# A bucket pass that shares its one-hot matrices between VectorE, TensorE and ScalarE, and a first hop in 128 columns

## Chip, cores and metric

One core of one Trainium2 chip. The metric is the device time of one execution in microseconds (us), the median of several runs. PE is TensorE, DVE is VectorE, ACT is ScalarE, POOL is GpSimd and SP is SyncE, whose queue issues most of the DMAs.

## What is computed

A graph of N = 10000 nodes with E = 160000 random edges and D = 128 features. Seven hops propagate the features over the edges; a small attention block then runs over the eight values of each node.

```python
h = x
toks = [x]
for _ in range(7):
    msg = h[src] * deg_inv_sqrt[src, None] * deg_inv_sqrt[dst, None]
    h = _segment_sum(msg, dst, N)
    toks.append(h)
tok = jnp.stack(toks, axis=1)                      # (N, 8, D)
...                                                # attention over the 8 tokens of a node
return jnp.einsum('nk,nkd->nd', alpha, o)
```

The change touches only how the edges are sorted and how the first hop is summed.

## The kernel before

**Sorting.** Gather and scatter are done as matrix products with one-hot matrices. For this the edges are bucketed twice. The first pass (`pass_a`) sorts them by destination block, 79 blocks of 128 nodes. The second pass sorts each block's edges by source block: 72 cells with 32 slots each, in 18 groups of four cells (NG = 18), and one more group of four cells (NI = 1) for the sources of the last blocks, so NJ = 19 groups of 128 slots. Edges that don't fit go through an overflow list.

**The second pass, in quads.** Four destination blocks make a quad; there are 20. `place` sorts a quad in two pairs of blocks. For each pair DVE makes the one-hot `oh` of the source cells (L417), PE counts with 25 identity matmuls into `ur` (L421), ACT copies the counts as `H` (L422), four triangular matmuls sum them (L427), ACT copies this as `U` (L429), DVE multiplies `ux` (L219), 16 + 1 matmuls add (L223, L224), DVE reduces to the ranks `rk` (L227), makes the one-hot of the rank `rob` and two products `R` with the source and the destination row (L434, L435), and 50 matmuls put both into the table `tb` (L440), which ACT copies to `tbs` (L441). Then the quad's source rows are stored to DRAM (`srow`, L450), PE spreads the destination rows over partitions with small selection matmuls (L454), ACT copies them as `dsl` (L458), DVE takes the indices `oidx` (L459), and the overflow list is made with `po`, `ph`, two one-hots `ohp` (L484) and matmuls (L487), ending in `lo` and `Sov` (L490 to L494).

**`matrices`** makes the matrices of a block in one fp8 tile `w` of 128 x 4736: 18 groups of gather matrices by comparing `rb` with the partition's number (L511; `rb` is the block's `srow` row on all 128 partitions, loaded at L504 into a pool with one buffer), and 19 scatter matrices of 128 x 128 by comparing `dsl` with a running number (L514). `w` is stored to DRAM for the later hops (L516).

**`hop1` and `block`** use `w` at once for the first hop. For each of nine pairs of groups, `gather` issues eight matmuls that write 32 partitions each into a PSUM tile `p` (L580; pool of three banks), and the tile is copied to `eb`, by ACT (L585) except in the last quad, where it is shared with DVE (L587). A table row is 256 columns wide, two f16 halves whose sum is the value. `scat` multiplies the scatter matrices with `eb` into `acc` (L556), 256 columns and one of ones, which counts in-degrees. `fetched` does it for rows that POOL fetched by indirect DMA (L542). `close` adds the two halves with a DVE reduction into `s` (L571), and `fin1` and `token_out` read `s` (L652, L623).

**The order.** The main loop runs `place` of quad q+1, `matrices` of quad q and `hop1` of quad q-1 side by side. A scheduler then orders the instructions of each engine at build time; on the chip each engine takes them strictly in that order. Hops 2 to 7 load `w` from DRAM and run only `block`.

Of the kernel before, what the change touches and what calls it, by code (L numbers as in the profile page):

```python
# [35 lines left out]
KO = 8  # L36
BIG = 32768.0


class Hops:  # L40
    def __init__(self, ctx, dp, missing, tab, tc, x, src, dst, dis):
# [9 lines left out]
        self.srow = dp.tile([NTP, 4 * NG * CAP], F16, name="srow")  # L51

# [51 lines left out]
        self.mx = [cp.tile([128, NT], F32, name=f"mx{i}") for i in range(2)]  # L104
        self.ctok = [cp.tile([128, NT], F32, name=f"ctok{i}") for i in range(2)]
        self.c1 = [cp.tile([128, NT], F32, name=f"c1{i}") for i in range(2)]
# [289 lines left out]
    def pb_open(self, c):  # L396
        tc, V = self.tc, self.nc.vector
        self.bwp = c.enter_context(tc.tile_pool(name="bw", bufs=2))
        self.bw1 = c.enter_context(tc.tile_pool(name="bw1", bufs=1))
        self.pU = c.enter_context(tc.tile_pool(name="pU", bufs=1, space=PSUM))  # L400
        self.psm = c.enter_context(tc.tile_pool(name="psm", bufs=1, space=PSUM))

        cp = self.bp
        es = cp.tile([NS, 4, NJ], I32, name="es")
        self.nc.gpsimd.iota(es, pattern=[[1, 4], [4, NJ]], base=0, channel_multiplier=-1)
        self.esel = cp.tile([NS, 4, NJ], F16, name="esel")
        V.tensor_scalar(self.esel, es, 0.0, None, op0=ALU.is_equal)

    def place(self, ts, got):
# [41 lines left out]
        dsl = wp.tile([128, 4, NJ], F16, name="dsl")  # L451
        for g in range(n):
            for q in range(4):
                T.matmul(msc[32 * q:32 * q + 32, 32 + g * NJ:32 + (g + 1) * NJ], tbs[:, g, CAP:2 * CAP], self.esel[:, q, :],  # L454
                         start=True, stop=True, tile_position=(0, 32 * q))
                T.matmul(msc[32 * q:32 * q + 32, 16 + g * NI:16 + (g + 1) * NI], tbs[:, g, 0:CAP], self.esel[:, q, NG:],
                         start=True, stop=True, tile_position=(0, 32 * q))
        A.copy(dsl[:, :n, :], msc[:, 32:32 + n * NJ].rearrange("p (g j) -> p g j", j=NJ))  # L458
# [38 lines left out]
    def matrices(self, ts, dsl, W):  # L497

        nc, V = self.nc, self.nc.vector

        def row(t):
            rb = self.bw1.tile([128, 4 * NG * CAP], F16, name="rb")
            r1 = self.srow[t:t + 1, :]
            nc.sync.dma_start(rb, bass.AP(tensor=r1.tensor, offset=r1.offset, ap=[[0, 128], [1, 4 * NG * CAP]]))  # L504
            return rb

        rb = row(ts[0])
        yield
        for g, t in enumerate(ts):
            w = self.gsp.tile([128, (NJ + NG) * 128], F8, name="w")  # L510
            V.tensor_scalar(w[:, NJ * 128:], rb, self.pid1, None, op0=ALU.is_equal, saturate=False)  # L511
            if t != ts[-1]:
                rb = row(t + 1)
            V.tensor_tensor(w[:, :NJ * 128].rearrange("p (j d) -> p j d", d=128), dsl[:, g, :, None].to_broadcast([128, NJ, 128]),  # L514
                            self.iof1[:, None, :].to_broadcast([128, NJ, 128]), op=ALU.is_equal, saturate=False)
            nc.sync.dma_start(self.GSd[t], w)  # L516
            W.append(w)
            yield
# [11 lines left out]
    def block(self, t, w, tab, og, pend, lag, runs, first, evac, fin, lead=False, late=False, mid=None, ahead=None,  # L530
# [5 lines left out]
        m = 257 if first else 256  # L536
        acc = []


        def fetched(i, start=False, stop=False):  # L540
            W = w[:, (NG + i) * 128:(NG + i + 1) * 128] if i < NI else self.Sov[:, t, :]
            T.matmul(acc[0][:, :256], W, og[i], start=start, stop=stop)  # L542
            if first:
                T.matmul(acc[0][:, 256:257], W, self.ones16, start=False, stop=False)
# [6 lines left out]
        def scat(e, jj):  # L551
            if not acc:
                acc.append(self.pacc.tile([128, 512], F32, name="acc", tag="acc"))
            for j in range(e.shape[1]):
                J = 2 * jj + j
                T.matmul(acc[0][:, :m], w[:, J * 128:(J + 1) * 128], e[:, j, :m], start=first and J == 0,  # L556
                         stop=J == NG - 1 and not (first or late))
                if first and J == 0 and not lead:
                    for i in range(NI):
                        fetched(i)  # L560

        def close():
            if first:
                if lead:
                    for i in range(NI):
                        fetched(i)
                T.matmul(acc[0][:, 256:257], self.Sov[:, t, :], self.ones16, start=False, stop=False)
            if first or late:
                T.matmul(acc[0][:, :256], self.Sov[:, t, :], og[NI], start=False, stop=True)  # L569
# [59 lines left out]
    def run(self, ctx, att, nhop=K):  # L629
        tc, nc, V, A, T, G = self.tc, self.nc, self.nc.vector, self.nc.scalar, self.nc.tensor, self.nc.gpsimd  # L630
        with ExitStack() as c:
# [16 lines left out]
            def fin1(t, s, acc):  # L648
                V.tensor_copy(self.indeg[:, t:t + 1], acc[:, 256:257])  # L649
# [48 lines left out]
        with ExitStack() as c:  # L698
# [5 lines left out]
            self.sp = c.enter_context(tc.tile_pool(name="sp2", bufs=2))  # L704
            self.more_ebufs(c.enter_context(tc.tile_pool(name="eb2", bufs=1)), 9, False)
# [592 lines left out]
```

## Time and profile before

| | |
|---|---|
| median of 3 runs | 3991.8 us (3988.98 to 3993.97) |
| the profiled execution | 3999.62 us, its span 3997.8 us |
| mean granted TensorE clock | 0.973 |
| busy over the span | PE 94%, DVE 83%, ACT 68%, POOL 44% |
| first pass | about 0 to 370 us |
| second pass with the first hop | about 370 to 1190 us |
| hops 2 to 7 | about 1190 to 3310 us |
| attention | to the end |

A row of a group gives the line, the engine, the operation, the tiles (out<-in), the shapes and the count; behind the first bar the busy time in us and the mean of one in ns; behind the second the idle time of the engine just before these instructions and what ended it. A row of a timeline gives the start in us, the length in us, and in brackets the idle time before it. A row of the waits gives the total in us, how often, and the longest. A row of the windows gives the start and end of a stretch, its length, then busy us and instructions of PE, PEld (weight loads), DVE, ACT and POOL, the granted clock, the DMA share and GB/s.

### The profile page before, as it was taken

The numbers are of one execution on the slowest core, as the hardware profiler recorded it, in microseconds if no ns is written. First come the engines' busy times: TensorE is split into PE (matmuls) and PEld (weight loads), VectorE is DVE, ScalarE is ACT, GpSimd is POOL, SyncE is SP. The second block draws the span as 40 slices with busy tenths as digits, with TensorE's granted clock in tenths as the row PEclk, the third lists the DMA queues.
The fourth block names the chain that finished last, engine by engine and source line by source line (L and its number), as shares of the span: only waits on it lengthen the run. The fifth ranks groups of instructions, "written<-read, shape, count | busy, mean of one in ns | idle before, by whom it ended". The sixth has DMA issues, their size and how long they took to land.

```text
span 3997.8 us, 165094 instructions
## 1 busy us (share of the span) xinstructions
PE 3745.5 (94%) x69690; PEld 3031.4 (76%) x69690; DVE 3322.9 (83%) x6961; ACT 2724.5 (68%) x6830; POOL 1766.6 (44%) x2342
## 2 busy tenths in 40 slices
PE   6886799999989999999999999999999999999997
PEld 4665566666658888888888788878878887788885
DVE  8998999999977777777777777777766666999998
ACT  6884456666666666666666666666665658888884
POOL 0000333333335665666666566656656662222222
PEclk8998899999999999999999999999999999999998
DMA  3100445454556666666666666666656552222220
GB/s 104 32 2 1 134 151 154 149 162 143 156 168 189 201 201 193 202 203 200 193 202 202 185 202 202 202 189 198 202 184 205 186 183 77 74 74 76 78 78 13
DMA packets 321189, 594.93 MB, mean 149 GB/s; under 512 B 56183, under 2 KB 214101, under 8 KB 315189
## 3 DMA queue, kind: packets, MB, share of 16 engines
q1 hardware_dynamic: 282485, 506.62, 40.0%
q0 software_dynamic: 35392, 72.55, 6.3%
q8 instruction: 546, 8.95, 0.9%
q10 hardware_dynamic: 2560, 5.12, 0.4%
q14 instruction: 206, 1.69, 0.1%
HBM read 455.43 MB, written 128.67 MB: 146 GB/s over the span
## 4 chain that ended last, share of the span: by engine, by line
PE 71%; DVE 19%; ACT 4%; issue 2%; DMA 2%; POOL 0%; another core or an unknown queue 0%; SPq 0%; DVEq 0%; ACTq 0%; POOLq 0%
PE p L580 26%; PE acc L556 24%; PE acc L542 4%; DVE w L514 3%; PE pv L972 3%; PE po L983 3%; PE pu L961 3%; DVE ux L219 2%; DVE o L212 2%; ACT rs L340 2%; PE tb L440 2%; PE pt L951 1%; DVE oh L206 1%; DVE R L212 1%; DVE w L511 1%
## 5 line engine op out<-in xcount | busy, mean ns | idle before, releaser
L585 ACT CAST eb<-p 128x512 f16<-128x512 f32 x3065 | 1623.7, 596 | 645.4 <-PE p L580 404.3
L587 DVE TENSOR_TENSOR eb<-p,one 128x512 f16<-128x512 f32 x1912 | 1230.6, 685 | 332.2 <-PE acc L556 195.9
L580 PE MATMUL p<-tab,w 128*32 128x256 f16 x39816 | 1288.7, 274 | 44.2 <-issue 21.4
L556 PE MATMUL acc<-eb,w 128*128 128x256 f16 (+1 forms) x9954 | 1246.9, 274 | 8.4 <-DVE indeg L649 3.1
L580 PEld LDWEIGHTS <-w 128*32 128x32 fp8e4 x39816 | 1002.3, 96 | 261.3 <-issue 225.8
L556 PEld LDWEIGHTS <-w 128*128 128x128 fp8e4 x9954 | 954.3, 98 | 170.3 <-issue 54.9
L526 POOL DMA_INDIRECT og<-tabh,oidx x553 | 613.3, 1109 | 767.7 <-DVE vi L478 389.6
L526 POOL DMA_INDIRECT og<-tabd,oidx x541 | 586.3, 1084 | 640.2 <-PE acc L556 294.3
L625 POOL TENSOR_SCALAR r<-s,ctok 128x128 f32<-128x128 f32 x474 | 294.3, 621 | 47.7 <-DVE s L571 30.3
L616 ACT ACTIVATE tab<-s,c 128x128 f16<-128x128 f32 x395 | 158.6, 402 | 209.7 <-DVE eb L587 185.6
L617 DVE SCALAR_TENSOR_TENSOR tab<-s,c,tab 128x128 f16<-128x128 f32 x395 | 138.9, 352 | 180.8 <-issue 168.0
L571 DVE TENSOR_REDUCE s<-acc 128x128 f32<-128x256 f32 x553 | 228.7, 414 | 24.0 <-PE acc L569 11.2
L997 ACT ACTIVATE junk<-tab 128x128 f32<-128x128 f32 x625 | 245.1, 394 | 0.0
L340 ACT ACTIVATE rs<-iof,rb 128x128 fp8e4<-128x128 f32 x784 | 231.8, 389 | 0.3
L514 DVE TENSOR_TENSOR w<-dsl,iof 128x2432 fp8e4<-128x2432 f16 x79 | 211.5, 2678 | 0.0
L983 PEld LDWEIGHTS po<-v,pT 128*128 128x128 f32 x1250 | 159.5, 194 | 42.1 <-issue 27.7
L525 POOL COPY og<-eb 128x1 f16<-128x1 f16 x452 | 83.9, 186 | 241.7 <-ACT eb L585 241.7
L1055 POOL TENSOR_TENSOR p<-e,in 128x512 f32<-128x512 f32 (+1 forms) x40 | 40.8, 1020 | 321.0 <-DVE e L1053 321.0
L972 PE MATMUL pv<-Wv,xT 128*128 128x131 f32 x1250 | 176.7, 285 | 1.3 <-ACT xT L952 0.6
L983 PE MATMUL po<-v,pT 128*128 128x128 f32 x1250 | 167.0, 277 | 5.5 <-DVE tab L989 4.1
L972 PEld LDWEIGHTS pv<-Wv,xT 128*128 128x128 f32 x1250 | 154.2, 192 | 17.9 <-issue 8.8
L542 PE MATMUL acc<-og,w 128*128 128x256 f16 x553 | 156.8, 284 | 0.0
(285 smaller groups left out, 4611.9 us busy)
## 6 DMA issues: line engine op xcount, KB each, us to landing
w<-gsd SPq DMA_DIRECT2D x474, 592.0 KB
gsd<-w SPq DMA_DIRECT2D x79, 592.0 KB
rb<-srow SPq DMA_DIRECT2D x79, 576.0 KB
tok<-r SPq DMA_DIRECT2D x546, 64.0 KB
tab<-tok SPq DMA_DIRECT2D x273, 128.0 KB
tabd<-tab SPq DMA_DIRECT2D x396, 64.0 KB
og<-tabh,oidx POOLq DMA_INDIRECT x553
og<-tabd,oidx POOLq DMA_INDIRECT x541
```

The source lines that it names most:

```text
L340: A.activation(ro[:, j - a, i, :], self.iof, AF.Abs_reciprocal_sqrt, scale=2.0 ** 21, bias=rb[:, j - VP, i:i + 1], saturate=False)
L514: V.tensor_tensor(w[:, :NJ * 128].rearrange("p (j d) -> p j d", d=128), dsl[:, g, :, None].to_broadcast([128, NJ, 128]), self.iof1[:, None ...
L526: self.nc.gpsimd.indirect_dma_start(out=o, out_offset=None, in_=src[0] if i == NI else src[1], in_offset=bass.IndirectOffsetOnAxis(ap=self ...
L542: T.matmul(acc[0][:, :256], W, og[i], start=start, stop=stop)
L556: T.matmul(acc[0][:, :m], w[:, J * 128:(J + 1) * 128], e[:, j, :m], start=first and J == 0, stop=J == NG - 1 and not (first or late))
L580: T.matmul(p[32 * q:32 * q + 32, j], w[:, NJ * 128 + s * CAP:NJ * 128 + (s + 1) * CAP], tab[:, s, :], start=True, stop=True)
L585: A.copy(e[:, :n, 0:256], pv)
L587: V.tensor_tensor(e[:, :n, 0:256], pv, self.one[:, :, None].to_broadcast([128, n, 256]), op=ALU.mult)
L625: self.nc.gpsimd.tensor_scalar(r, s, ct[:, t:t + 1], None, op0=ALU.mult)
L972: T.matmul(p[:, g - a, :], S[i]["xT"][:, g, :], Wv, start=True, stop=True)
L983: T.matmul(p[:, g - a, :], PT[i % 2][:, g, :], S[i]["v"][:, g, :128], start=True, stop=True)
L997: A.activation(j, S[i]["x"][:, g, :], AF.Square, bias=S[i]["x"][:, g, 0:1], scale=-1.0, accum_out=S[i]["sq"][:, g:g + 1])
```

## The change

Twelve of the 19 scatter matrices of a block (NX = 12) are no longer made by DVE's comparison. The quad's destination rows are stored to DRAM (`drow`) and loaded per block as four partitions of a small tile `dT`, whose fifth partition holds ones. One matmul with the constant `diff` (selectors, and minus the running number) gives the difference of destination row and running number for four matrices in one PSUM tile of 512 columns. It comes from the same pool and tag as the gathers' `p`. ACT turns it into fp8 with 1 / sqrt(|2^21 d + 1|), which is 1 where the difference is zero and rounds to zero elsewhere. DVE makes the other seven matrices as before.

In the first hop the two halves of a row are multiplied by two matmuls of 128 columns that add into the same 128 columns of `acc`, so that the sum stands in PSUM and the reduction falls away; ACT reads `acc` itself. The column of ones goes from 256 to 128.

The tiles mx0, ctok1 and the two c1 are taken in the pool of hops 2 to 7.

```diff
@@ place
         nc.sync.dma_start(self.srow[a:b, :]..., tbs[:4 * NG, :n, 0:CAP])
-        dsl = wp.tile([128, 4, NJ], F16, name="dsl")
+        nc.sync.dma_start(self.drow[a:b].rearrange("t j (q r) -> (j q) t r", r=CAP), tbs[:4 * NX, :n, CAP:2 * CAP])
+        nd = NJ - NX
+        dsl = wp.tile([128, 4, nd], F16, name="dsl")
@@ matrices
             nc.sync.dma_start(rb, bass.AP(tensor=r1.tensor, offset=r1.offset, ap=[[0, 128], [1, 4 * NG * CAP]]))
-            return rb
+            dT = self.dT[t % 2]
+            nc.sync.dma_start(dT[1:], self.drow[t].rearrange("(g j) p -> j g p", j=4))
+            return rb, dT
...
-            V.tensor_scalar(w[:, NJ * 128:], rb, self.pid1, None, op0=ALU.is_equal, saturate=False)
+            V.tensor_scalar(w[:, NJ * 128:], rb[0], self.pid1, None, op0=ALU.is_equal, saturate=False)
+            for j in range(0, NX, 4):
+                x = self.pg.tile([128, 4, 128], F32, name="x", tag="p")
+                T.matmul(x, rb[1][:, j // 4, :], self.diff, start=True, stop=True)
+                A.activation(w[:, j * 128:(j + 4) * 128], x.rearrange("p j d -> p (j d)"), AF.Abs_reciprocal_sqrt, scale=2.0 ** 21,
+                             bias=self.one, saturate=False)
             if t != ts[-1]:
                 rb = row(t + 1)
-            V.tensor_tensor(w[:, :NJ * 128]..., dsl[:, g, :, None].to_broadcast([128, NJ, 128]), ...)
+            V.tensor_tensor(w[:, NX * 128:NJ * 128]..., dsl[:, g, :, None].to_broadcast([128, NJ - NX, 128]), ...)
@@ block
+        def both(W, rows, start, ones):
+            T.matmul(acc[0][:, :128 + ones], W, rows[:, 128:256 + ones], start=start, stop=False, skip_group_check=True)
+            T.matmul(acc[0][:, :128], W, rows[:, :128], start=False, stop=False, skip_group_check=True)
...
-                T.matmul(acc[0][:, :m], w[:, J * 128:(J + 1) * 128], e[:, j, :m], ...)
+                if first:
+                    both(w[:, J * 128:(J + 1) * 128], e[:, j], J == 0, 1)
...
-                T.matmul(acc[0][:, 256:257], self.Sov[:, t, :], self.ones16, start=False, stop=False)
-            if first or late:
+                fetched(NI, stop=True)
+                fin(t, acc[0][:, :128], acc[0])
+                return
+            if late:
@@ fin1
-                V.tensor_copy(self.indeg[:, t:t + 1], acc[:, 256:257])
+                V.tensor_copy(self.indeg[:, t:t + 1], acc[:, 128:129])
```

More of the change, by code (lines that the diff above doesn't have):

```diff
@@ L36 @@
 KO = 8
+NX = 12
 BIG = 32768.0
@@ L555, in scat @@
                 J = 2 * jj + j
-                T.matmul(acc[0][:, :m], w[:, J * 128:(J + 1) * 128], e[:, j, :m], start=first and J == 0,
-                         stop=J == NG - 1 and not (first or late))
+                if first:
+                    both(w[:, J * 128:(J + 1) * 128], e[:, j], J == 0, 1)
+                else:
+                    T.matmul(acc[0][:, :256], w[:, J * 128:(J + 1) * 128], e[:, j, :256], start=False, stop=J == NG - 1 and not late)
                 if first and J == 0 and not lead:
@@ L704, in run @@
             self.sp = c.enter_context(tc.tile_pool(name="sp2", bufs=2))
+            lp = c.enter_context(tc.tile_pool(name="lp2", bufs=1))
+            self.mx[0], self.ctok[1] = (lp.tile([128, NT], F32, name=z) for z in ("mx0", "ctok1"))
+            self.c1 = [lp.tile([128, NT], F32, name=f"c1{i}") for i in range(2)]
             self.more_ebufs(c.enter_context(tc.tile_pool(name="eb2", bufs=1)), 9, False)
```

37 lines of the change are left out of this document (23 added, 14 removed).

## Prediction

> **What bounds the kernel now.** First the page's slices, which give the stages:
>
> ```profile
> span 3997.8 us, 165094 instructions
> ...
> PE   6886799999989999999999999999999999999997
> ...
> DVE  8998999999977777777777777777766666999998
> ACT  6884456666666666666666666666665658888884
> ...
> GB/s 104 32 2 1 134 151 154 149 162 143 156 168 189 201 201 193 202 203 200 193 202 202 185 202 202 202 189 198 202 184 205 186 183 77 74 74 76 78 78 13
> ```
>
> Each digit is 100 us. DVE is at 9 from slice 5 to slice 10 and falls to 7 at slice 11: that stretch is the second bucket pass with the first hop, the only stage that the diff touches. Hops 2 to 7 (PE at 9) and the attention read the same matrices as before, so the sum is made in this stage alone. The windows and the waits of DVE in its steady part:
>
> ```profile
> core 0: us, PE busy (x) PEld busy (x) DVE busy (x) ACT busy (x) POOL busy (x), PEclk, DMA share, GB/s
> 500.00:1100.00 600.00, 547.04 (x9710) 402.81 (x9706) 582.88 (x851) 371.33 (x813) 219.08 (x123) 0.98 0.49 153
> ```
>
> ```profile
> DVE oidx L459 <- ACT dsl L458: 12.0, 15, 1.1
> ...
> DVE w L511 <- DMA rb<-srow: 1.5, 2, 1.0
> ```
>
> DVE works 582.88 of 600 us and its longest wait is 12.0 us in all. DVE sets the pace; PE's 547.04 holds pipeline drains, so it is no bound. What DVE does there (mean ns in the second figure after the bar):
>
> ```profile
> L514 DVE TENSOR_TENSOR w<-dsl,iof 128x2432 fp8e4<-128x2432 f16 x62 | 165.9, 2677 | 0.0
> L511 DVE TENSOR_SCALAR w<-rb,pid 128x2304 fp8e4<-128x2304 f16 x62 | 87.3, 1408 | 1.8 <-DMA rb<-srow 1.5 <-issue 0.3
> L219 DVE TENSOR_TENSOR ux<-oh,U 128x3800 f16<-128x3800 f16 x31 | 65.8, 2124 | 0.0
> L206 DVE TENSOR_TENSOR oh<-kB,io 128x3800 f16<-128x3800 f16 x31 | 65.8, 2123 | 0.0
> L206 DVE TENSOR_TENSOR ohp<-ph,io 128x2048 f16<-128x2048 f16 x30 | 36.5, 1216 | 0.4 <-PE acc L567 0.4
> ...
> L206 DVE TENSOR_TENSOR rob<-rk,io 128x1600 f16<-128x1600 f16 x31 | 30.3, 979 | 0.0
> L571 DVE TENSOR_REDUCE s<-acc 128x128 f32<-128x256 f32 x61 | 24.9, 408 | 0.0
> ```
>
> The natural unit is a quad (4 blocks, one round of placing). There are two `ux` in a quad, so 31 are 15.5 quads, and a quad takes 600 / 15.5 = 38.7 us, of which DVE works 582.88 / 15.5 = 37.6.
>
> **The change, part by part.** *Taken from DVE.* L514 goes from 2432 to 896 elements. The rows with 1600 and 3800 elements give a fixed part of 147 ns, so L514 costs (2677 - 147) / 2432 = 1.04 ns an element and 896 cost 1.08 us: 1.60 saved a block. (By the 0.52 ns an element of the f16 rows it would be 0.61; the output stays fp8, so I take 1.08.) L571 goes: its successors start about 0.08 us before its end, so 0.33 a block. A quad saves 4 x 1.93 = 7.7 us, and DVE's work falls to 37.6 - 7.7 = 29.9. If nothing else were late, that is the gain. Conversely, **the change loses time as soon as DVE waits more than 38.7 - 29.9 = 8.8 us in a quad.** So the question is what DVE waits for.
>
> The engines take their instructions in program order, and the changed program has a new one. In 15 of its 20 quads it reads (a quad has two placing pairs; `x` are the new difference matmuls, `X` ScalarE's roots, `e` the evictions of gathers, W1 the comparison with `rb`, W2 the rest of the scatter matrices):
>
> ```
> DVE ... R R v W1 W2 | oh ux W1 W2 tab mx rk rob v R R v (8 small)
>     | oh oidx W2 po po ph ohp ohp W1 lo oidx Sov W2 W1 tab mx ux rk rob v R R v W1 W2
> PE  after oh of pair 2: 4 ur matmuls, 50 tb matmuls of pair 1, 21 ur, 16 gathers, 8 scatter,
>     24 gathers, 12 scatter, 4 triangle matmuls, 3 x
> ACT tbs | H e e e e e U X X X ...
> ```
>
> Before, W1, W2 and the reduction stood between `oh` and `ux`, and other work between `ux` and `rk`. Now these are neighbours. What the chain between them costs, from the timeline:
>
> ```profile
> 804.43 2.00 PE L440 MATMUL tb<-R,oh 128*76 128x64 f16 x50 [1.01 <-DVE R L212]
> 806.26 0.28 PE L556 MATMUL acc<-eb,w 128*128 128x257 f16 x1
> ...
> 806.51 1.04 PE L556 MATMUL acc<-eb,w 128*128 128x257 f16 x8
> ...
> 808.32 1.81 PE L421 MATMUL ur<-oh,id 128*128 128x152 f16 x25
> ...
> 810.50 0.25 PE L427 MATMUL ur<-H,triw 128*128 128x38 f16 x4
> ```
>
> ```profile
> 806.15 2.12 DVE L206 TENSOR_TENSOR oh<-kB,io 128x3800 f16<-128x3800 f16 x1
> ```
>
> ```profile
> 806.88 2.05 ACT L585 CAST eb<-p 128x512 f16<-128x512 f32 x4
> 810.16 0.29 ACT L422 CAST H<-ur 128x152 f16<-128x152 f32 x1 [1.23 <-PE ur L421]
> 810.79 0.29 ACT L429 CAST U<-ur 128x152 f16<-128x152 f32 x1 [0.34 <-PE ur L427]
> ```
>
> ```profile
> 832.92 1.27 PE L223 MATMUL ur<-ux,id 128*128 128x250 f16 x10
> ...
> 835.05 0.23 PE L224 MATMUL ur<-wB,id 128*128 128x50 f16 x1
> ```
>
> *Wait 1, `ux` behind `oh` (pair 2).* From the end of `oh` (808.27) PE starts at once (808.32): 0.05; 25 ur matmuls of (1.81 - 0.16 drain) / 25 = 0.066 us: 1.65; the 50 tb matmuls between them hold PE for 806.26 - 804.43 = 1.83; drain and hand-over 0.2; H about 0.2; five evictions, which start (2.05 - 0.59) / 3 = 0.487 apart (0.59 is the length of one): 2.43; U and hand-over 0.34. Sum **6.7 us**, with DVE idle. The gathers that feed the evictions hide the triangle matmuls and the scatter. Before, this chain ran from 808.27 to 811.08, 2.8 us, under W2 and W1.
>
> *Wait 2, `rk` behind `ux` (pair 1).* 15 matmuls that start (1.27 - 0.28) / 9 = 0.11 apart and two of 50 columns, with drain and hand-over: **2.1 us**.
>
> These two alone make 8.8, all that was saved. Two more come from `rb`, which has one buffer and so is loaded only after the W1 before it. Its latency, and the size of a store that now stands ahead of it:
>
> ```profile
> 1135.22 0.32 SPq L450 DMA_DIRECT2D srow<-tbs  x1
> ...
> 1136.81 0.37 SPq L504 DMA_DIRECT2D rb<-srow  x1
> ...
> 1143.90 0.67 SPq L504 DMA_DIRECT2D rb<-srow  x1
> ```
>
> ```profile
> gsd<-w SPq DMA_DIRECT2D x79, 592.0 KB
> ```
>
> ```profile
> 494.59 0.33 SPq L504 DMA_DIRECT2D rb<-srow  x1
> ```
>
> ```profile
> 499.22 1.42 DVE L511 TENSOR_SCALAR w<-rb,pid 128x2304 fp8e4<-128x2304 f16 x1 [1.04 <-DMA rb<-srow]
> ```
>
> ```profile
> 1149.30 1.42 DVE L511 TENSOR_SCALAR w<-rb,pid 128x2304 fp8e4<-128x2304 f16 x1 [1.96 <-DMA rb<-srow]
> ```
>
> From issue to the W1 that waited: 499.22 - 494.59 = 4.6 us, and 1149.30 - 1143.90 = 5.4. From the store of `srow` to the load that reads it: 1.6.
>
> *Wait 3, the first W1 of a quad.* From the end of R (pair 2): tb 2.0, tbs 0.3, srow to rb 1.6, rb 4.6 to 5.4 = 8.5 to 9.3. DVE's work in that time, with the numbers above: `v` and eight small 1.1, `oh` 2.05, oidx and W2 1.15, po and ph 0.3, two ohp 2.3 = 6.9. Wait 1.6 to 2.4; the changed queue has a store of w and the new `drow` store ahead of this load, worth up to 3 more (592 KB at the 202 GB/s that the GB/s row reaches). I take **2.5**.
>
> *Wait 4, the second W1 right after.* Between it and the first stand only lo, oidx, Sov and W2, 1.8 us, against 4.6 to 5.4. I take **3.3** (2.8 to 3.9 with hand-overs).
>
> Sum of waits: 6.7 + 2.1 + 2.5 + 3.3 = 14.6. A quad: 29.9 + 14.6 = **44.5**, 5.8 more than before.
>
> *Added elsewhere, hidden.* ScalarE gets 12 roots of 512 columns a quad; the nearest rows:
>
> ```profile
> L652 ACT ACTIVATE y<-s,dis 128x128 f32<-128x128 f32 x61 | 24.7, 405 | 58.6 <-DVE s L571 58.4 <-issue 0.2
> ...
> L157 ACT ACTIVATE tab<-y,q 128x256 f16<-128x256 f32 x31 | 15.5, 500 | 0.0
> ```
>
> 405 at 128 and 500 at 256 columns continue to 0.69 at 512, started some 0.6 apart; four times the first row, 1.62, is the upper end, the eviction's 0.59 the lower. ACT then works 371.33 / 15.5 + 12 x 0.6 = 31.2 of 44.5 us. Three roots stand between H and U of pair 1. From the second ohp on, DVE needs 2.5 + 1.3 + 1.8 + 3.3 + 1.3 + 0.7 = 10.9 us to the `ux` that reads this U; PE and ACT need about 1.4 (ohp's matmuls and scatter) + 1.7 (23 ur) + H 0.2 + roots 1.8 + four evictions 1.95 + y, r, tab 1.0 + U 0.3 = 8.4. At 1.62 a root it would be 0.5 late.
>
> PE gets 12 matmuls of 512 columns (0.22 each at L223's rate, 2.7 a quad) and two matmuls of 128 columns for one of 256. Rows: 152 columns every 66 ns, 64 every 37 (L440), so 128 about 58: 116 against 109 for the pair (L556, eight in 1.04), 0.6 us for 80 pairs of a quad, while PE waits anyway. The Trainium skill speaks against this edit: "TensorE: Matmul & The Clock Gate", section "Back-to-back issue gap", gives 81 ns sustained for weights plus 128 columns. By it a pair would be 162 ns and PE would have 4.2 us more in a quad; the trace's 66 ns for 152 columns with weights loaded each time does not bear it out. With a sixth of that on DVE's chain, as in rival C, an estimate by that page is 13 us on top of my sum.
>
> The DMAs of `dT` (four a quad, 0.32 us of SP each) are issued a block ahead; behind them wait rb loads, inside waits 3 and 4. The store of w now waits for ACT too. `acc` is freed by ACT's two reads instead of DVE's reduction, with a second bank as cover; without it, about 2 us a block. The moved tiles (mx0, ctok1, c1) cost nothing before hop 2.
>
> **The sum.** 15 quads x 5.8 = 87; three early quads have half of the pattern, 9; the first two (no hop) and last two quads -5 (DVE is shorter there, between -13 and +5, where rb paces the blocks as before). Together +91. The profiled execution took 3999.6 us (span 3997.8), 7.8 above the median of 3991.8; 3999.6 + 91 = 4090.6, and from the median **4083 us**. Low end: no wait 3, 2.8 for wait 4, gives 2.8 x 15 = 42, less 13: 4021. High end: wait 3 at 5.4, wait 4 at 3.9, waits 1 and 2 together a us longer: 49.0 a quad, 10.3 x 15 + 20 = 175: 4167.
>
> **Rivals.** *A, faster: the waits stay under 8.8 us a quad.* This is the point from which the sign turns. It needs rb early enough (waits 3 and 4 gone) and a wait 1 well under 6.7. With half, 4.4: 15 x -4.4 - 5 = -71, 3921 us. For it: DVE waits almost nowhere today and ACT has room for its 31.2. Against it: `oh` and `ux` are neighbours and nothing on PE or ACT can overtake. Chance 0.08.
>
> *B, about equal: rb never late.* Waits 1 and 2 eat just what was saved: 3992, give or take 20. Against it: 1.8 us of work between two W1 and no rb seen under 4.6. Chance 0.06.
>
> *C, slower still: a 128-column scatter matmul costs its weight load.* The weight rows of the page,
>
> ```profile
> L556 PEld LDWEIGHTS <-w 128*128 128x128 fp8e4 x9954 | 954.3, 98 | 170.3 <-issue 54.9
> ```
>
> have 98 ns; two would be 196 for 109, and the 20 between ur and the triangle matmuls would then outlast the five evictions by 0.4, with others in front of `rk` some 1.2 us a quad: 18 x 1.2 = 22, 4105 us. Against it the 66 ns above. Chance 0.12.
>
> **How the numbers follow.** Forecast 0.74. Faster: A and a third of B, 0.10; within 0.2% (what a measurement here can tell from no change): 0.03; slower: 0.87. The range 4015 to 4165 holds most of the forecast's bounds and C.
>
> **What would show it.** DVE's share in the stage falls from 97% to about 67% and the stage is some 90 us longer. Waits of DVE: `ux` for ACT's U about 100 us in all (15 x 6.7), `rk` for PE 30, W1 for rb 87. Evictions keep 0.59, roots 0.6 to 0.7, scatter pairs about 116 ns. I am wrong if DVE stays above 90%, if rb waits are under 20 us, or if the gap between `oh` and `ux` is under 4 us.

## The result and the profile after

The changed kernel takes 4025.36 us (median of 4 runs, 4021.89 to 4027.3) against 3992.2 us (4 runs beside it): ratio 1.0078, 95% interval 1.0062 to 1.0094. It is 33 us slower, in the forecast's direction and inside its range, but the forecast was 91 us.

First the page's slices of the changed kernel, the same rows as were shown of before:

```profile
span 4025.2 us, 169111 instructions
...
PE   6887899999999999999999999999999999999997
...
DVE  8998777777757777777777777777776665999998
ACT  6884577777776666666666666666665667888884
...
GB/s 105 31 2 1 146 149 142 146 150 149 149 172 161 198 202 192 202 200 201 193 198 203 188 207 202 200 190 201 202 192 200 187 186 84 74 73 73 78 79 13
```

From slice 5 on DVE is at 7 where it was at 9, and ACT at 7 where it was at 6; DVE's 5 is the slice with the stage's last blocks. The steady stretch, from the windows:

```profile
500.00:1100.00 600.00, 578.92 (x10666) 414.39 (x10664) 465.21 (x761) 446.27 (x955) 169.78 (x118) 0.99 0.46 148
```

PE is busy 578.92 of 600 us (547.04 before), DVE 465.21 (582.88), ACT 446.27 (371.33). The waits of DVE in it, then those of PE:

```profile
DVE rk L228 <- PE ur L225: 33.1, 15, 3.4
DVE ux L220 <- ACT U L439: 31.9, 15, 2.7
DVE oh L207 <- PE tb L450: 19.6, 16, 1.3
DVE w L533 <- PE acc L560: 17.4, 15, 1.8
DVE w L525 <- DMA rb<-srow: 16.2, 18, 1.6
DVE ohp L207 <- PE msc L499: 9.1, 14, 0.7
```

```profile
PE p L609 <- ACT eb L614: 8.3, 26, 0.4
PE ur L224 <- DVE ux L220: 8.0, 9, 1.6
```

DVE now waits for everybody, and PE for almost nobody: with three rows of 1.1, 0.8 and 0.2 us its waits come to 18.4 us of 600. The pace has passed from DVE to PE. The profile's chain of work that ended last says the same of this stretch: of the rows that it lists, PE's make 61.6% of the time (26.9% before) and DVE's 9.5% (51.1% before). The loads of `rb` make 10.8%, so DVE's wait for them is not wholly off the path.

How much longer a quad is, and where the 33 us lie, is read best from the `indeg` copy, which DVE makes once for each of the 79 blocks. Here are the 1st, 9th, 69th and 79th in the timeline of before, then of after:

```profile
454.46 0.15 DVE L649 COPY indeg<-acc 128x1 f32<-128x1 f32 x1
...
539.49 0.15 DVE L649 COPY indeg<-acc 128x1 f32<-128x1 f32 x1
...
1122.84 0.14 DVE L649 COPY indeg<-acc 128x1 f32<-128x1 f32 x1
...
1183.98 0.15 DVE L649 COPY indeg<-acc 128x1 f32<-128x1 f32 x1
```

```profile
451.72 0.15 DVE L678 COPY indeg<-acc 128x1 f32<-128x1 f32 x1
...
540.23 0.15 DVE L678 COPY indeg<-acc 128x1 f32<-128x1 f32 x1
...
1146.44 0.15 DVE L678 COPY indeg<-acc 128x1 f32<-128x1 f32 x1
...
1217.70 0.15 DVE L678 COPY indeg<-acc 128x1 f32<-128x1 f32 x1
```

From the 9th to the 69th are 15 quads: 583.35 us before and 606.21 after, 38.89 and 40.41 a quad, so +22.9 us in all. Up to the 9th it is +0.7. From the 69th to the end it is 61.14 and 71.26, +10.1. The sum, 33.7, is the difference of the last copies (1217.70 - 1183.98) and stands beside the 33 us of the medians. From there to the end of the span the two take 2813.8 and 2807.5 us, and another profile of the kernel before, before_again, takes 2809.6: that part is the same but for some us by which profiles of one kernel differ.

The last ten blocks lose nearly as much as seven quads of the steady part. The windows of that end, before and then after:

```profile
1133.00:1184.00 51.00, 45.13 (x787) 28.08 (x785) 38.68 (x73) 35.12 (x75) 15.89 (x12) 1.00 0.58 194
```

```profile
1176.00:1186.00 10.00, 8.56 (x165) 5.18 (x156) 4.34 (x8) 9.19 (x20) 4.83 (x3) 1.00 0.56 179
1186.00:1196.00 10.00, 9.34 (x180) 5.99 (x172) 0.93 (x3) 8.74 (x19) 2.01 (x3) 1.00 0.74 224
...
1156.00:1218.00 62.00, 55.97 (x1080) 37.96 (x1069) 29.40 (x56) 47.97 (x102) 17.83 (x15) 0.97 0.54 173
```

There the ranking comes to its end and DVE has room (0.93 of 10 us in one window). Before, it worked 38.68 of the 51 us, on the matrices too; now it works 29.40 of 62, and ACT, with the roots and the evictions, 47.97, about 9 of 10 in two of the windows. PE works 55.97 of the 62 us. Work was moved away from the engine that falls free at the end. Whether ACT or PE makes the end longer these rows don't decide; experiment 2 does.

### The profile page after: what moved, and what is told of

Same layout as the page of the kernel before. It is cut to its first block, busy times and chain, and to the rows that moved or that the text cites. A ratio compares the mean times of both kernels' runs of the same rounds, so it can differ in the third digit from the quotient of the medians.

```text
span 4025.2 us, 169111 instructions
## 1 busy us (share of the span) xinstructions
PE 3816.7 (95%) x71507; PEld 3075.5 (76%) x71507; DVE 3203.1 (80%) x6886; ACT 2847.4 (71%) x7067; POOL 1716.4 (43%) x2343
## 3 DMA queue, kind: packets, MB, share of 16 engines
q1 hardware_dynamic: 287861, 507.11, 40.2%
## 4 chain that ended last, share of the span: by engine, by line
PE 71%; DVE 19%; DMA 5%; ACT 3%; issue 2%; SPq 0%; another core or an unknown queue 0%; DVEq 0%; POOL 0%; POOLq 0%; ACTq 0%
PE p L609 27%; PE acc L584 23%; PE acc L569 4%; DVE o L213 2%; DMA rb<-srow 2%; PE tb L450 2%; PE ur L224 2%; DVE st L1110 2%; DVE oh L207 2%; DVE ux L220 2%; PE acc L559 2%; PE pv L1004 1%; DVE tab L1021 1%; PE po L1015 1%; PE acc L560 1%
## 5 line engine op out<-in xcount | busy, mean ns | idle before, releaser
L609 PEld LDWEIGHTS <-w 128*32 128x32 fp8e4 x39816 | 989.5, 96 | 233.1 <-issue 177.5
L584 PE MATMUL acc<-eb,w 128*128 128x256 f16 x8532 | 1013.2, 273 | 0.0
L584 PEld LDWEIGHTS <-w 128*128 128x128 fp8e4 x8532 | 836.5, 98 | 98.7
L545 POOL DMA_INDIRECT og<-tabd,oidx x541 | 540.9, 1000 | 804.8 <-PE acc L567 453.2
L559 PE MATMUL acc<-eb,w 128*128 128x129 f16 x1422 | 215.0, 223 | 1.3 <-ACT eb L614 1.3
L600 DVE TENSOR_REDUCE s<-acc 128x128 f32<-128x256 f32 x474 | 196.8, 415 | 20.2 <-PE acc L598 14.2
L560 PE MATMUL acc<-eb,w 128*128 128x128 f16 x1422 | 210.5, 221 | 0.0
L559 PEld LDWEIGHTS <-w 128*128 128x128 fp8e4 x1501 | 139.0, 98 | 75.9 <-issue 75.9
L529 ACT ACTIVATE w<-x,one 128x512 fp8e4<-128x512 f32 x237 | 149.2, 689 | 62.8 <-PE x L528 60.3
```

Of the source, the lines that this page charges most:

```text
L545: self.nc.gpsimd.indirect_dma_start(out=o, out_offset=None, in_=src[0] if i == NI else src[1], in_offset=bass.IndirectOffsetOnAxis(ap=self ...
L559: T.matmul(acc[0][:, :128 + ones], W, rows[:, 128:256 + ones], start=start, stop=False, skip_group_check=True)
L560: T.matmul(acc[0][:, :128], W, rows[:, :128], start=False, stop=False, skip_group_check=True)
L584: T.matmul(acc[0][:, :256], w[:, J * 128:(J + 1) * 128], e[:, j, :256], start=False, stop=J == NG - 1 and not late)
L609: T.matmul(p[32 * q:32 * q + 32, j], w[:, NJ * 128 + s * CAP:NJ * 128 + (s + 1) * CAP], tab[:, s, :], start=True, stop=True)
```

## The experiments

**Two theories.** P: PE paces the changed stage, and what is added to PE, or taken from it, comes out in the time. D, the prediction's: DVE's chain of waits (on `U`, on `ur`, on `rb`) paces it, and PE has room. A third, C, was that the 128-column matmuls cost their weight load.

The kernel before, run beside each of these kernels, took 3991 to 3995 us for some of them and 3939 to 3941 us for the others. They are called the slower and the faster group below, and each ratio is to the kernel before of the same runs. The expectations speak of chips; the chip's number on record is 7 or 4 in the slower group and 11, 13 or 4 in the faster one, so the number does not tell the groups apart, and that the chip is the cause is not shown. Each edited kernel is also scheduled anew, so its engines' orders can differ in more than the edit. The table puts the quad (from the 9th to the 69th `indeg`), the work of PE and DVE in it (busy time of 500 to 1100 us, scaled to the quad) and the last `indeg` side by side; the text goes through the runs.

| kernel | ratio (95%) | quad | PE | DVE | last indeg |
|---|---|---|---|---|---|
| slower group: before | 1 | 38.9 | 35.5 | 37.8 | 1184.0 |
| after | 1.0078 (1.0062 to 1.0094) | 40.4 | 39.0 | 31.3 | 1217.7 |
| x_twice | 1.0180 (1.0159 to 1.0201) | 42.4 | 41.2 | 31.3 | 1257.4 |
| half_scatter | 0.9980 (0.9971 to 0.9989) | 38.4 | 35.8 | 31.5 | 1172.2 |
| matrices_only | 1.0068 (1.0055 to 1.0081) | 40.2 | 38.7 | 32.7 | 1212.1 |
| split_only | 1.0007 (0.9997 to 1.0017) | 39.1 | 36.0 | 37.0 | 1185.6 |
| rb_two | 1.0066 (1.0052 to 1.0079) | 39.9 | 38.9 | 31.4 | 1207.6 |
| split_rb | 0.9943 (0.9929 to 0.9956) | 37.6 | 35.2 | 36.9 | 1156.0 |
| runs333 | 1.0262 (1.0248 to 1.0276) | 44.3 | 41.1 | 31.7 | 1285.8 |
| faster group: before_b | 1 | 37.9 | 35.0 | 37.7 | 1163.3 |
| after_again | 1.0111 (1.0097 to 1.0126) | 40.1 | 38.8 | 31.3 | 1211.7 |
| nx8 | 1.0062 (1.0048 to 1.0075) | 38.6 | 37.4 | 33.3 | 1189.2 |
| nx4 | 1.0023 (1.0014 to 1.0032) | 37.3 | 35.5 | 34.8 | 1163.5 |
| nx4_rb_b | 1.0008 (0.9998 to 1.0017) | 37.2 | 35.3 | 35.0 | 1162.1 |
| runs3033_b | 1.0109 (1.0095 to 1.0124) | 39.9 | 38.3 | 31.7 | 1206.2 |
| oh_one | 1.0210 (1.0194 to 1.0226) | 40.9 | 39.0 | 31.1 | 1249.1 |

**1. More work for PE alone: each difference matmul twice.**

```diff
-                T.matmul(x, rb[1][:, j // 4, :], self.diff, start=True, stop=True)
+                for _ in range(2):
+                    T.matmul(x, rb[1][:, j // 4, :], self.diff, start=True, stop=True)
```

> Edit: each difference matmul of the changed kernel is issued twice into the same PSUM tile (12 more matmuls of 512 columns in a quad, 0.25 us each by the changed kernel's trace, 3.0 us). Theory P (PE paces the changed stage: PE works 39.1 of the 40.6 us of a quad): the whole 3.0 us shows, 18 quads x 3.0 = 54, about 4079 us. Rival D (the chain of waits of DVE paces it, as the prediction had it, and PE has room): at most 0.5 us a quad, under 4036 us.

4065.54 us, ratio 1.018. The windows of this kernel:

```profile
500.00:1100.00 600.00, 582.29 (x10343) 415.43 (x10344) 442.36 (x716) 430.83 (x914) 195.41 (x112) 0.97 0.43 141
```

PE stays at 97% and the quad grows by 2.0 us for 12 more matmuls, 0.17 us each. PE's work grows by 2.2 us (39.0 to 41.2) and not by the 3.0 expected; nearly all of that comes out in the time, which D excludes. P holds, with less than it expected.

**2. Less work for PE: the low halves left out of the first hop.**

```diff
             T.matmul(acc[0][:, :128 + ones], W, rows[:, 128:256 + ones], ...)
-            T.matmul(acc[0][:, :128], W, rows[:, :128], ...)
```

> Edit: the second of the two 128-column scatter matmuls of the first hop is left out, so the low halves of the rows are missing from the first hop's sums; everything else of the changed kernel stays. 80 matmuls less in a quad, 56 ns each, 4.5 us. Theory P: a quad falls from 40.6 to about 36.5 (then DVE and ACT with 31 us of work each and their waits are near), 18 x -4.1 = -74, about 3951 us. Rival D: DVE's waits stay, a quad at 40, above 4010 us.

3984.87 us, ratio 0.998. The time falls by 1% against the changed kernel, so P has the direction; but only by about half of what it expected. The waits of PE in this kernel say why:

```profile
PE p L608 <- ACT w L529: 14.8, 52, 0.8
PE p L608 <- ACT eb L613: 14.5, 30, 0.6
```

With 35.8 us of work PE waits for ACT, which holds the PSUM tiles `p` and `x` for evictions and roots (466.63 of 600 us busy). PE is the pace-setter with little to spare behind it.

This run also tells what makes the last ten blocks longer. From the 69th to the last `indeg`, in the changed kernel and in this one:

```profile
1146.44:1217.70 71.26, 65.29 (x1266) 44.99 (x1257) 36.68 (x75) 55.01 (x116) 20.33 (x17) 0.98 0.51 164
```

```profile
1108.62:1172.21 63.59, 56.34 (x1051) 33.78 (x1047) 36.36 (x75) 54.03 (x116) 19.53 (x17) 0.97 0.58 183
```

PE has 9.0 us less to do and the stretch is 7.7 us shorter, though ACT and DVE work as before. In the kernel before PE works 54.1 of its 61.1 us there. So PE sets the pace of the end too, and ACT's load is not the reason.

**3. One half of the change at a time.** `matrices_only` undoes the split first hop (256 columns and the reduction as before), `split_only` keeps the split hop and lets DVE make all 19 matrices:

```diff
matrices_only, scat:
-                if first:
-                    both(w[:, J * 128:(J + 1) * 128], e[:, j], J == 0, 1)
+                T.matmul(acc[0][:, :m], w[:, J * 128:(J + 1) * 128], e[:, j, :m], ...)
split_only, matrices:
-            for j in range(0, NX, 4):
-                ...
-            V.tensor_tensor(w[:, NX * 128:NJ * 128]..., dsl[:, g, :, None].to_broadcast([128, NJ - NX, 128]), ...)
+            V.tensor_tensor(w[:, :NJ * 128]..., dsl[:, g, :, None].to_broadcast([128, NJ, 128]), ...)
```

> Edit: only the twelve matrices from TensorE and ScalarE; the first hop as before (one scatter matmul of 257 columns, halves added by DVE). Theory P: PE loses only 80 x 4 ns = 0.3 us a quad against the changed kernel, 4015 to 4025 us: the matrices carry the loss. Rival C (two matmuls of 128 columns cost far more than one of 257): half or more of the 33 us lost comes back, under 4010 us. Rival D: DVE gets 1.3 us a quad more work on its chain, 4045 us.

> Edit: only the first hop's split into 128 columns; all 19 matrices by DVE as in the kernel before. Theory P: PE stays at 35.4 of a quad and does not pace; DVE, which paces there, loses 1.3 us of 37.8 a quad, 18 x -1.3 = -23, about 3969 us, faster than both. Rival C: PE would be the bound, about 3992 us or more.

4021.28 us and 3994.17 us, ratios 1.0068 and 1.0007. The matrices carry nearly the whole loss, the split hop none: C has fallen. But split_only misses the gain that P expected. The waits of DVE in it:

```profile
DVE w L511 <- DMA rb<-srow: 20.1, 21, 2.1
DVE tab L158 <- ACT tab L157: 10.3, 15, 1.3
```

The time that the reduction had filled is waited away at the one `rb` buffer.

**4. How many matrices.** NX = 8 and NX = 4 in place of 12:

```diff
-NX = 12
+NX = 8
```

> Edit: eight matrices instead of twelve come from TensorE and ScalarE (two difference matmuls a block), the split stays. Theory P: PE loses 1.0 us a quad against the changed kernel, 40.6 to 39.6, 18 x -1.0 = -18, about 4007 us. Rival D: DVE gets 2.1 us a quad more work on its chain, slower than the changed kernel, 4060 us.

> Edit: four matrices come from TensorE and ScalarE, the split stays. Theory P: PE at 36.4 with about 1.5 of waits, DVE at 34.4 a quad, about 37.9 against 38.5 before: 18 x -0.6 = -11, about 3981 us, between 3970 and 3995. Rival D: DVE's work rises by 4.3 us a quad against the changed kernel, above 4040 us.

3967.8 us and 3946.3 us, ratios 1.0062 and 1.0023, in the faster group; both lie above what P expected (4007 and 3981 beside 3992, or 1.004 and 0.997). The expectations had scaled 12 matrices' loss from the other group. Set against `after_again` (experiment 8) the step is even: 40.1, 38.6 and 37.3 us a quad with 12, 8 and 4 matrices, that is 1.3 to 1.5 us for four x matmuls of a quad, about 0.35 each, of which 0.25 is their spacing on PE. DVE's work rises as the time falls (31.3, 33.3 and 34.8 us), which D excludes. ACT's work falls with PE's here (30.1, 27.5 and 25.5 us), so these rows alone do not tell the two apart; x_twice does. With 4 matrices PE (35.5) and DVE (34.8) are level, the quad is 0.6 us under before, and the total still is not, because the end costs more: from the 69th to the last `indeg` 67.3 us, against 60.1 in before_b and 70.1 in after_again. The longer end comes mostly with the matrices (71.1 in matrices_only and 62.9 in split_only, beside 61.1 before), and four of them bring most of it. These steps are rough: the same stretch is 64.2 us in before_again, 3.1 more than in the other profile of that kernel. PE's work in it is 53.4 us in before_b, 59.3 with four matrices and 65.8 with twelve. Why four cost so much of it stays open.

**5. The lead of `oh` taken away.** In the changed kernel `oh` has two buffers; here it has one:

```diff
-            oh = self.onehot(wp, "oh", cols(self.kB), NS)
+            oh = self.onehot(w1, "oh", cols(self.kB), NS)
```

> Edit: the one-hot oh has one buffer instead of two, so that DVE cannot make it ahead and the next product ux has to wait through the whole chain on PE and ACT, as the prediction had assumed. If the chain was sized rightly (6.7 us for that wait), DVE's work 31.4 + 6.7 + 2.1 + the other waits of the trace 2.9 = 43.1 us a quad, 15 x 2.5 = 38 more than the changed kernel, about 4063 us, and the trace shows ux waiting about 100 us for ACT's U in all. If PE still paces (P without this chain), about 4025 us and a wait of some 30 us.

4023.23 us, ratio 1.021, in the faster group: 37 us more than `after_again`, where the chain had been expected to cost 38 and P nothing. That the sum comes out near 38 is chance, as its parts show. DVE's wait of `ux` for `U` is 47.2 us in 15 times, 3.1 each, where the changed kernel has 2.1; so the lead of one pair does shorten wait 1, though even without it the wait is under half of the forecast 6.7. Of the loss against `after_again` (37 us by the last `indeg`) only 0.8 us a quad, 12 in all, lie in the steady part; 24 are a start that comes later (first `indeg` at 475.19 instead of 451.27). From 375 us to that first copy DVE waits 34.5 us for `U`, `ur` and `tb`, and 6.1 in `after_again`: so ahead of the first hop, with one buffer, the chain does cost time. As the scheduler put many instructions elsewhere in this kernel, this run shows less than it was meant to.

**6. The disputed waits on `rb` taken away.** Two `rb` buffers, in the changed kernel and with the split hop alone (the pair one-hot `ohp` shares a buffer with `R`, for the space):

```diff
-            rb = self.bw1.tile([128, 4 * NG * CAP], F16, name="rb")
+            rb = self.bw1.tile([128, 4 * NG * CAP], F16, name="rb", bufs=2)
```

> The changed kernel with two rb buffers in place of one (the pair one-hot shares a buffer that is there, for the space), so that the next W1 need not wait for a load that the last W1 released. Theory P (TensorE paces the changed stage: it was busy 578.9 of 600 us there and waited 21): VectorE's 16 us of waits on rb go, but the end moves by at most what TensorE waited: 0 to 15 us under the changed kernel, 4010 to 4025 us beside 3992, ratio 1.004 to 1.009. Theory D (the prediction's: waits 3 and 4 on rb cost 5.8 us a quad on the path): 87 us under the changed kernel, 3938 us, ratio 0.987.

> The kernel before with the split first hop alone and two rb buffers. VectorE paces it (it was busy 567.6 of 600 us with the split alone, and waited 20.1 us on rb there). Theory P (the single rb buffer took what the split gave): VectorE's work of a quad falls from 37.8 to about 36.6 us and nothing takes its place, so 1.2 x 15 = 18 us less than before, 3974 us, ratio 0.995. Rival: the wait on tab (10.3 us with the split alone) or another takes the place of rb's, 3990 to 3994 us, ratio 1.000.

`rb_two` takes 4021.04 us, ratio 1.0066: D's 3938 us is refuted. The wait on `rb` falls from 16.2 to 7.7 us, the quad by 0.5 us, and PE is even busier. The quad so gains what the wait lost (8.0 us in 15 quads for 8.5): DVE's waits are not all hidden behind PE, though they are worth far less than D has them.

```profile
500.00:1100.00 600.00, 585.67 (x10817) 418.67 (x10816) 471.72 (x767) 453.39 (x973) 162.28 (x119) 0.99 0.46 151
```

`split_rb` takes 3972.61 us, ratio 0.9943 (0.9929 to 0.9956), as P had it: DVE still paces, with less to do, and nothing takes the place of the wait (5.0 us of `rb` in all):

```profile
500.00:1100.00 600.00, 561.63 (x11298) 441.21 (x11296) 588.04 (x816) 374.67 (x838) 264.03 (x127) 1.00 0.48 158
```

It beats both kernels, by 0.6% and 1.3%, in the slower group, where it was run.

**7. Fewer switches between gather and full-array matmuls.** The trace of after has 32-column gathers and 128-column matmuls some 0.1 us further apart where one kind follows the other than among themselves, so I tried the nine gather units of a block in three runs instead of four:

```diff
-                    yield from self.block(t, w, self.tab[0], og, pend, 2, (2, 2, 2, 3), True,
+                    yield from self.block(t, w, self.tab[0], og, pend, 2, (3, 3, 3), True,
```

> The changed kernel with the gather matmuls of a first-hop tile dealt out in three runs of 3 units in place of four (2, 2, 2, 3): the same matmuls, with one switch fewer between 32-column gather matmuls and full-array ones in each tile. Theory P (TensorE paces, and a switch there and back costs it about 0.2 us): 4 x 0.2 = 0.8 us a quad, 10 to 15 us under the changed kernel, 4010 to 4015 us beside 3992, ratio 1.005. Theory D (VectorE's waits pace, TensorE has room): no change, ratio 1.0078, or more, since a gathered group comes later.

4099.57 us, ratio 1.0262: slower by 1.8% than the changed kernel, against both theories. The run had changed a second thing. A block now takes three steps of the main loop instead of four, so a quad's hop is through after 12 of its 16 steps, and the ranking's last steps stand on PE without gathers or scatter between them. PE's waits, then the windows of a stretch at that place:

```profile
PE msc L499 <- DVE ohp L207: 28.1, 26, 2.0
```

```profile
826.00:828.00 2.00, 0.81 (x24) 0.59 (x20) 0.70 (x3) 1.22 (x4) 0.94 (x1) 1.00 0.79 310
828.00:830.00 2.00, 0.97 (x18) 0.68 (x19) 2.00 (x2) 0.09 (x1) 0.00 (x0) 0.77 0.27 75
830.00:832.00 2.00, 2.00 (x19) 0.67 (x18) 2.00 (x7) 1.81 (x4) 0.00 (x0) 0.50 0.21 81
832.00:834.00 2.00, 2.00 (x31) 1.17 (x30) 2.00 (x2) 1.49 (x4) 0.48 (x1) 0.50 0.98 384
834.00:836.00 2.00, 2.00 (x32) 1.49 (x20) 2.00 (x2) 1.56 (x3) 2.00 (x1) 0.53 0.60 209
```

Where PE works 1.78 of 4 us, the granted clock (third figure from the end) falls to 0.50 for the next six. Over the stretch it is 0.88 against 0.99. How the loss divides between the lost cover and the clock was not tried. The clean form keeps four steps and makes one of them empty:

```diff
-                    yield from self.block(t, w, self.tab[0], og, pend, 2, (2, 2, 2, 3), True,
+                    yield from self.block(t, w, self.tab[0], og, pend, 2, (3, 0, 3, 3), True,
```

> The changed kernel with the 9 gather units of a first-hop tile dealt 3, 0, 3, 3 over its four steps in place of 2, 2, 2, 3: one gather run fewer in each tile, and as many steps, so that the ranking's steps keep their cover (the runs of 3, 3, 3 took four of sixteen steps away). Theory P (TensorE paces; a switch between 32-column gather matmuls and full-array ones costs it about 0.2 us): 4 x 0.2 = 0.8 us a quad less, 12 us under the changed kernel, ratio 1.0045 to 1.0065 beside 1.0078. Rival (the switches are hidden, or what is saved is waited for): ratio 1.007 to 1.009.

3988.86 us, ratio 1.0125, in the faster group, and so not to be compared with the 1.0078.

**8. The same within one group.** The two kernels, unchanged, the last one, and four matrices with two `rb` buffers. That last had been run before, with 3944.68 us, ratio 1.001 (1.0001 to 1.0018), and with the empty step too, with 3948.73 us, 1.0018 (1.0008 to 1.0029); P had expected 0.992 and 0.989. Its edit (`ohp` shares `R`'s buffer here too):

```diff
nx4_rb, against the changed kernel:
-NX = 12
+NX = 4
...
-            rb = self.bw1.tile([128, 4 * NG * CAP], F16, name="rb")
+            rb = self.bw1.tile([128, 4 * NG * CAP], F16, name="rb", bufs=2)
```

> The changed kernel with 4 of 19 matrices by TensorE and ScalarE in place of 12, and two rb buffers. Theory P (the quad is the larger of VectorE's and TensorE's work): VectorE 36.6 less 2.2 (four matrices at 0.55) = 34.4 us, TensorE 35.1 + 1.0 (one x of 4 matrices a tile, 0.25 each) + 0.3 = 36.4 us a quad, some 2 us under the quad before: 30 us less, 3962 us beside 3992, ratio 0.992. Rival (VectorE's waits on the ranking's chain set the quad whatever TensorE does): as with one rb buffer, ratio 1.002.

> 4 of 19 matrices, two rb buffers, and the gather units dealt 3, 0, 3, 3. Theory P: TensorE paces nx4_rb, so the 0.8 us a quad of fewer switches comes off there too, 12 us, ratio 0.989. Rival: VectorE's waits set the quad, and the ratio is that of nx4_rb.

> The kernel before, unchanged, for a profile on this chip: both theories expect 38.5 us a quad (scaled by this chip's time) and VectorE as the busiest engine of the stage.

> The changed kernel, unchanged, beside runs3033 and the kernel before on one chip. If a chip's speed scales every stage alike, the ratio is 1.0078 again on any chip; if the faster chip of some of these runs gains its 1.3% in what VectorE paces and not in what TensorE paces, the ratio there is 1.010 to 1.013, and runs3033's 1.0125 is no loss against it.

> The gather units dealt 3, 0, 3, 3 again, now beside the changed kernel on one chip. Theory P with a price of 0.2 us a switch: 12 us under after_again. Rival (the price is hidden in waits, or is no price of TensorE's at all): within 4 us of after_again, or over it.

> The kernel before, unchanged, for a profile on the chip of this call: VectorE busy over 95% of the stretch from 500 to 1100 us, as on the first chip, and 38.5 us a quad if that stage takes the same time on every chip.

> 4 of 19 matrices and two rb buffers again, beside the changed kernel and the kernel before on one chip. If its 1.001 was of the kernel: 4 us over the kernel before, and 27 us under after_again. If it was of the chip: its quad of 37.4 us stands 1 us under the quad of before, 15 us less than before, ratio 0.996.

Measured: after_again 3986.35 us, ratio 1.0111; runs3033_b 3983.56 us, 1.0109; nx4_rb_b 3943.56 us, 1.0008; the kernel before alone, one run each, 3998.25 us in the slower group (before_again, 39.1 us a quad) and 3938.96 us in the faster (before_b, 37.9). The windows of before_b, after_again and runs3033_b, one kernel each:

```profile
500.00:1100.00 600.00, 553.91 (x9967) 409.42 (x9967) 596.25 (x872) 376.90 (x830) 236.17 (x126) 0.99 0.50 155
```

```profile
500.00:1100.00 600.00, 580.62 (x10764) 418.18 (x10762) 468.95 (x762) 450.45 (x967) 177.41 (x118) 0.99 0.46 149
```

```profile
500.00:1100.00 600.00, 575.27 (x10826) 420.41 (x10824) 476.08 (x770) 448.83 (x969) 219.25 (x118) 0.99 0.46 150
```

Three things follow. First, the faster group gains 1.0 us a quad in the kernel before and 0.3 in the changed one, and the change costs 47.6 us there and 33 in the other: ratios don't carry over between the two. In the faster group DVE works 596.25 of 600 us before the change and waits for next to nothing; what it waits 12.0 us for in the slower one (`oidx` for `dsl`) is 0.3 us here. Second, the switches save nothing: PE is busy 0.5 us a quad less in runs3033_b and the time is the same, the rest being waits on ACT and DVE. That P expected 12 us was wrong; PE's time is the bound only to within the 1 to 2 us by which most quads of the table stand above it. Third, four matrices with two `rb` buffers shorten the quad by 0.7 us and end where before ends (1162.1 against 1163.3): no gain, the last ten blocks taking 65.4 us instead of 60.1.

## Why the prediction was right in sign and wrong in size

*What paced the kernel before: right.* DVE did, and in the faster group it shows with hardly a wait.

*"PE's 547.04 holds pipeline drains, so it is no bound": this is the step that failed.* PE had 35.5 us of a 38.9 us quad. The prediction itself gives what comes on top, 2.7 us of x matmuls and 0.6 of pairs, and 35.5 + 3.3 = 38.8 is what PE has in the changed kernel (39.0). That fills the quad of before (38.9): by PE alone the change had nothing to gain, and with the 1.4 us that PE still waits the quad is 40.4. The prediction put the 3.3 us at nothing ("while PE waits anyway") and took its 44.5 from DVE's work and waits alone. The drains (a 128-column matmul is 0.22 us long, and the next starts after 0.056) are in the busy time both before and after, so they are no room for more work. x_twice and half_scatter show that the time follows PE's work, and the row of 12, 8 and 4 matrices agrees; how PE's figure splits into single switches and drains stays open.

*The sign: right, but in part by luck.* The argument for it was that DVE's waits pass 8.8 us a quad. They are 9.1, hardly more, and mostly they are waits for PE, which sets the pace (79 of the 127 us in the six rows of DVE's waits above).

*Sizes of what was added: right.* The x matmuls start 0.25 us apart with their surroundings (three in 802.36 to 803.11; 0.22 was forecast) and the 128-column matmuls every 56 ns, so a pair is 0.112 us (0.116). From PE's timeline of the changed kernel:

```profile
799.46 0.22 PE L560 MATMUL acc<-eb,w 128*128 128x128 f16 x1
799.51 0.22 PE L559 MATMUL acc<-eb,w 128*128 128x129 f16 x1
...
800.02 0.22 PE L560 MATMUL acc<-eb,w 128*128 128x128 f16 x1
...
802.36 0.81 PE L528 MATMUL x<-diff,dT 5*128 5x512 f16 x3
803.11 0.23 PE L559 MATMUL acc<-eb,w 128*128 128x129 f16 x1
```

From 799.46 to 800.02 are ten such matmuls, and the windows count as many weight loads as matmuls (10664 and 10666). The Trainium skill ("TensorE: Matmul & The Clock Gate", section "Back-to-back issue gap") sets 81 ns for them in a sustained stream and 56 for a single one; in this trace the stream has the 56, and matrices_only shows nothing to be won by undoing the split. ScalarE's root was forecast at 0.69 us and DVE's seven matrices at 1.08:

```profile
L529 ACT ACTIVATE w<-x,one 128x512 fp8e4<-128x512 f32 x178 | 112.7, 688 | 40.0 <-PE x L528 37.8
```

```profile
L533 DVE TENSOR_TENSOR w<-dsl,iof 128x896 fp8e4<-128x896 f16 x59 | 64.0, 1086 | 17.4 <-PE acc L560 17.4
```

DVE's work fell by 6.5 us a quad, not 7.7, to 31.3. The lengths of its instructions, added up, did fall by 7.7 (42.2 to 34.5 us). But the next instruction starts before the one ahead of it ends only where the two stand back to back, and with the waits between them the time so saved fell from 4.5 to 3.2 us a quad.

*Wait 1, `ux` behind `oh`, 6.7 us: wrong, it is 31.9 / 15 = 2.1.* The two are neighbours on DVE, but not of the same pair. From the timeline of all engines in the changed kernel:

```profile
815.75 0.43 PE L431 MATMUL ur<-oh,id 128*128 128x152 f16 x4
816.14 2.02 PE L450 MATMUL tb<-R,oh 128*76 128x64 f16 x50
...
817.99 1.55 PE L431 MATMUL ur<-oh,id 128*128 128x152 f16 x21
818.57 2.13 DVE L207 TENSOR_TENSOR oh<-kB,io 128x3800 f16<-128x3800 f16 x1
819.57 0.29 ACT L432 CAST H<-ur 128x152 f16<-128x152 f32 x1 [1.12 <-PE ur L431]
...
822.12 0.26 PE L437 MATMUL ur<-H,triw 128*128 128x38 f16 x4
822.58 0.30 ACT L439 CAST U<-ur 128x152 f16<-128x152 f32 x1
822.92 2.14 DVE L220 TENSOR_TENSOR ux<-oh,U 128x3800 f16<-128x3800 f16 x1 [2.22 <-ACT U L439]
```

The 25 `ur` matmuls that lead to this `ux` began at 815.75, before the `oh` of 818.57 that stands in front of it: `oh` has two buffers and is made a pair ahead. The prediction started the chain at the end of the wrong `oh`. What is left of the wait is H at 819.57, and then 2.3 us until PE, which is behind with gathers, comes to the triangle matmuls at 822.12: a wait on the pace-setter.

*Wait 2, `rk` behind `ux`, 2.1 us: right,* 33.1 / 15 = 2.2.

*Waits 3 and 4, on `rb`, 5.8 us a quad: wrong, 16.2 / 15 = 1.1.* The loads are about as slow as forecast (3.7 to 6.4 us from the issue to the W1 that waits for it, 4.6 to 5.4 in the prediction), but DVE meets other waits on the way (`oh` for `tb` 19.6 us in all, the second part of `w` for its buffer 17.4, `ohp` 9.1), in which `rb` lands. Waits on one engine don't simply add when they follow one another and a slower engine sits behind most of them. rb_two took half of this wait away and won 8 us in 15 quads. All together DVE waits 9.1 us a quad (40.4 - 31.3) instead of 14.6. Two of the three signs that the prediction named against itself came: rb waits under 20 us (16.2) and a gap between `oh` and `ux` under 4 us (2.22).

*"First two and last two quads -5": wrong in sign.* All up to the 9th block cost 0.7 us, where the three early quads alone had been put at 9, and the last ten cost 10.1. The prediction looked at DVE alone there, which has the room; PE has not (half_scatter).

*Rivals.* A fell with the sign. B's 3992, give or take 20, ended 13 us short of the result, though its condition, an `rb` that is hardly late, came near the truth. C fell with matrices_only.

## What to carry to other kernels

Before work is moved off the busiest engine, add what the receiving engines get to their own busy time of one round: here 35.5 + 3.3 already stood against 38.9. Waits found one by one on the relieved engine must not be added up; take the largest of the engines' sums first, and give the waits only what is left. And look at a stage's drain apart from its steady part: 10 of the 33 us are there, where the engine that was relieved is free in any case.

## What the runs showed of the hardware

- A stretch of 4 us in which TensorE worked 1.78 us, with two waits of 0.28 and 1.95 us, was followed by some 6 us at a granted clock of 0.50 (runs333). The Trainium skill ("TensorE: Matmul & The Clock Gate", section "HAM oscillation — how this bites in real kernels") warns of idle gaps over about 3.4 us; in this trace shorter ones were enough.
- The kernel before differs by 1.3% between the two groups (3991 to 3995 and 3939 to 3941 us), though its instructions last the same (`oh` 2126 ns in before_again and 2129 in before_b) and the mean clock is 0.974 and 0.978. Up to the last `indeg` it is 23.6 us (1186.94 and 1163.32) of the 59 us between these two. What differs was not found; chip number 4 stands in both groups.
